# Bias table by matmuls, fewer DMA transposes and another load order in a fused attention and feed-forward kernel

## The chip, the cores and the metric

The kernel runs on one core of a Trainium2 chip. The engines of the core work side by side, each on its own queue of instructions in the order in which the program wrote them: TensorE (PE, matrix products), VectorE (DVE), ScalarE (ACT), GpSimd (POOL) and SyncE (SP). SP and POOL here mostly issue DMAs. The metric is device time in microseconds, the median of several executions.

## The reference

Attention with a relative-position bias, followed by a two-layer network with a squared ReLU. Eight batches, eight heads, 576 positions, head width 64; then 4608 rows of width 512 and a hidden width of 2048.

```python
scores = scale * np.matmul(q, k.transpose(0, 1, 3, 2))        # scale = 1/8
bias = bias_table[bucket]              # bucket depends only on |i - j|; 32 buckets
scores = scores + bias.transpose(2, 0, 1)[None, :, :, :]
scores = scores - np.max(scores, axis=-1, keepdims=True)
attn = np.exp(scores)
attn = attn / (np.sum(attn, axis=-1, keepdims=True) + 1e-09)
attn_out = np.matmul(attn, v)
x = attn_out.transpose(0, 2, 1, 3).reshape(B * S, H * D)
h = np.maximum(x @ w_in, 0.0)
out = h * h @ w_out
```

From a distance of 128 on, all positions fall into the last bucket.

## The kernel before

**Attention, by pairs of heads.** There are 32 pairs, four to a batch (`pair`, L531). Scores are made transposed: keys on the partitions, queries along the row, so that exp(scores) can go into the product with v as the stationary operand. For this q and k must have the head width on the partitions. They are loaded with positions on the partitions (POOL issues these loads, which also convert to 16 bits, by the helper `loader`, L246) and turned in one of two ways. Below batch `DT_QK` = 2 PE turns them with an identity matrix (L559) and ACT or DVE copies the result out of PSUM (L522, L524). From batch 2 on SP issues DMA transposes (L543). Four small copies per pair (L586, on DVE or POOL) put the last 64 queries and keys into block-diagonal tiles `qz` and `kz`. Then PE makes the scores (L604, L628, L653), ACT the exponentials (L615, L638, L663), and PE the product with v (L734, L741); DVE takes the reciprocal of the row sums (L758) and normalises into the tile `x` (L763).

**The bias as a factor.** The bias is not added to the scores. DVE multiplies the exponentials by exp(bias - bias of the last bucket), which is 1 from distance 128 on, so only a band about the diagonal is multiplied (L696). The factors come from two tables with 128 rows, `tb_sb` (384 columns for each head) and `tm_sb` (192 columns for each pair of heads). They are built once at the start: SP loads the bias table, its last row and a one-hot matrix; DVE subtracts (L282), ACT takes the exponential (L285), one matmul makes the 8 x 512 vector of factors by distance (L289), DVE copies it (L296), SP writes it to DRAM and reads it back four times with one element of shift from partition to partition, and DVE copies the reversed rows into the tables (L320, L329).

**From attention to the network.** The network needs x with its 512 features on the partitions, `xt`. With `DT_X` true SP issues two DMA transposes for each pair (L779), three and two blocks of 128 rows. The other way, `x_turn` (L791), stands in the code but isn't used: after all four pairs of a batch, for each of five blocks of rows four PE transposes into one PSUM bank and one copy by ACT or DVE.

**The network, by groups of 512 rows.** Nine groups (`layers`, L830). The first layer is 16 x 4 matmuls of 512 columns (L897), each four followed by a ReLU on ACT (L918) and a square on DVE (L926). The second is 4 x 16 matmuls (L844), with a copy by ACT or DVE (L864, L870) and a store by SP (L878). The second layer of one group is interleaved with the first layer of the next. Both layers, the transposes and the table share three PSUM banks (`g_ps`).

**What sets the order.** The Python program doesn't issue instructions as it meets them. Each step is handed to a planner (`Plan`, L80) with an assumed duration on one or more engines, the steps that it needs, the buffers that it takes from rings, a due time and an earliest time. The planner simulates the engines: at each turn it takes the step that can start first, and by due time among equals; where a step allows two engines, the one that can start it first gets it. The instructions are then issued in the order of the planned starts (L953). So the assumed durations and due times decide which engine gets a copy, and the order of each engine's queue; on the chip the engines follow that order and wait for each other by semaphores. The due times come from `LEAD`, `FAST`, `FASTN` and `PERIOD` (pairs: `nominal`, L506), `AHEAD` (how long before its due time a pair may start) and `G0`, `GP` (groups of the network). DMA transfers are steps on a single planned engine "DMA", and DMA transposes on another, "XB".

**The loads.** POOL issues them in the order in which the program lists them (L481 to L502), as buffers allow: q and k of batch 0 by pairs with v between, the four parts of w_in, batch 1, the four parts of w_out, then batch by batch. q and k have two staging buffers, v has three.

Of the kernel before, what the change touches and what calls it, by code (L numbers as in the profile page):

```python
# [19 lines left out]
NBK = 32  # L20
# [155 lines left out]
def kernel(  # L176
# [17 lines left out]
    oh = np.zeros((NBK, 512), dtype=np.float16)  # L194
    oh[_bucket(np.abs(np.arange(512) - 256)), np.arange(512)] = 1.0
    oh_d = nc.inline_tensor(oh, name="c_oh")
    id_d = nc.inline_tensor(np.eye(128, dtype=np.float16), name="c_id")
    tdram = nc.dram_tensor("t_bias", (H, 512), FP16, kind="Internal")
# [12 lines left out]
    bt_sb = sb("bt_sb", [32, 8], FP32)  # L211
    far_sb = sb("far_sb", [32, 8], FP32)
    eb_sb = sb("eb_sb", [32, 8])
    tv_sb = sb("tv_sb", [H, 512])
    oh_sb = sb("oh_sb", [32, 512])
# [14 lines left out]
    tr_sb = gs[1][:, 0:6, :].rearrange("p a b -> p (a b)").rearrange("p (h w) -> p h w", h=H)  # L230
# [9 lines left out]
    r_set, r_pv, r_g = Ring(2), Ring(1), Ring(3)  # L240
# [5 lines left out]
    def loader(eng_name, eng, out_, in_, packets, deps=(), bufs=(), due=0.0):  # L246

        issue = P.add(
            {eng_name: 800.0 if eng_name == "POOL" else 60.0},
            lambda: io(eng.dma_start(out=out_(), in_=in_())),  # L250
            deps,
            bufs,
            due,
        )
        return P.add({"DMA": packets / 16}, None, [issue], bufs, due), issue
# [8 lines left out]
    nc.scalar.add_instruction(  # L264
        mybir.InstLoadActFuncSet(
            name=nc.get_next_instruction_name(),
            act_func_set_id=tabs.index("natural_log_exp_and_others"),
            ins=[],
            outs=[],
        )  # L270
    )

    l_bt = load("SP", nc.sync, const(bt_sb), const(bias_table), 32 * 27, due=0)
    l_far = load(
        "SP", nc.sync, const(far_sb), const(bias_table[NBK - 1 : NBK, :].to_broadcast([NBK, H])), 32 * 27, due=1
    )
    l_oh = load("SP", nc.sync, const(oh_sb), const(oh_d.ap()), 32 * 60, due=2)
    l_id = load("SP", nc.sync, const(id_sb), const(id_d.ap()), 128 * 27, due=3)

    o = P.add(  # L280
        {"DVE": 150.0},
        lambda: io(nc.vector.tensor_tensor(out=bt_sb, in0=bt_sb, in1=far_sb, op=mybir.AluOpType.subtract)),  # L282
        [l_bt, l_far],
    )
    o_eb = P.add({"ACT": 220.0}, lambda: io(nc.scalar.activation(out=eb_sb, in_=bt_sb, func=EXPF)), [o])  # L285
    bt_b = Buf(r_g)
    o = P.add(
        {"PE": 600.0},
        lambda: io(nc.tensor.matmul(g_ps[bt_b.slot][0:H, :], eb_sb, oh_sb, start=True, stop=True)),  # L289
        [o_eb, l_oh],  # L290
        [bt_b],
        mode="t",
    )
    o = P.add(
        {"DVE": 700.0},
        lambda: io(nc.vector.tensor_copy(out=tv_sb, in_=g_ps[bt_b.slot][0:H, :])),  # L296
        [o],
        [bt_b],
    )
    o = load("SP", nc.sync, lambda: tdram.ap(), const(tv_sb), 16 * 60, [o])  # L300
    l_rev = [
        load(
            "SP",
            nc.sync,
            const(tr_sb[:, 2 * c : 2 * c + 2, :]),
            const(bass.AP(tensor=tdram, offset=2 * c * 512 + 1, ap=[[1, 128], [512, 2], [1, 384]])),
            256 * 50,
            [o],
        )
        for c in range(4)  # L310
    ]
    l_tab = []
    for c in range(4):
        turned = tr_sb[:, 2 * c : 2 * c + 2, ::-1]
        l_tab.append(
            [
                P.add(
                    {"DVE": 900.0},
                    lambda c=c, turned=turned: io(
                        nc.vector.tensor_copy(out=tb_sb[:, 2 * c : 2 * c + 2, :], in_=turned)  # L320
                    ),
                    [l_rev[c]], (), 5000.0 * c,
                )
            ]
            + [
                P.add(
                    {"DVE": 320.0},
                    lambda c=c, e=e, turned=turned: io(
                        nc.vector.tensor_copy(out=tm_sb[ds(64 * e, 64), c, :], in_=turned[0:64, e, 0:192])  # L329
                    ),  # L330
                    [l_rev[c]], (), 5000.0 * c,
                )
                for e in range(2)
            ]
        )
# [57 lines left out]
    def load_six(b, w, h0, nh):  # L393
        src = (q, k)[w]
        l = load(
            "POOL", nc.gpsimd,
            lambda: six(stg[b_stg[b].slot][w])[:, h0 : h0 + nh, :],
            const(src[b, h0 : h0 + nh].rearrange("h (p j) d -> p h (j d)", j=6)),
            96 * nh * 107, (), [b_stg[b]], pdue(),
        )  # L400
        for hp in range(h0 // 2, (h0 + nh) // 2):
            l_qk[b, w, hp] = [l]
# [32 lines left out]
    def load_v_tail(b, hps):  # L435
# [10 lines left out]
    def load_v(b):  # L446
# [9 lines left out]
        load_v_tail(b, range(4))  # L456
# [4 lines left out]
    def load_w_in(u):  # L461
# [5 lines left out]
                512 * 140, (), (), pdue(),  # L467
# [3 lines left out]
    def load_w_out(u):  # L471
# [5 lines left out]
                512 * 140, (), (), pdue(),  # L477
# [10 lines left out]
    for h in range(4, 8):  # L488
        load_v_head(0, h)
    for u in range(4):  # L490
        load_w_in(u)
    for w in range(2):
        load_six(1, w, 0, 4)
    load_v(1)
    for w in range(2):
        load_six(1, w, 4, 4)
    for u in range(4):
        load_w_out(u)
# [13 lines left out]
    def one_of(engs, fn, deps, bufs, due):  # L512
        op = P.add(engs, None, deps, bufs, due)
        op.fn = lambda: fn(op)
        return op

    def copy_to(engs_n, out_f, in_f, deps, bufs, due, fp16=True):


        def emit():  # L520
# [5 lines left out]
        op = P.add(  # L526
            {"DVE": dve(engs_n, 2.0 if fp16 else 1.0, 140.0), "ACT": act(engs_n)}, emit, deps, bufs, due
        )
        return op

    def pair(p):  # L531
# [5 lines left out]
        for w, dst in ((0, qts), (1, kts)):  # L537
            if b >= DT_QK:
# [9 lines left out]
                evac.append(P.add({"XB": 800.0}, None, [o], [qb, b_stg[b]], T - 6000))  # L548
# [29 lines left out]
            evac.append(copy_to(S, straight, turned, [o], [bank, qb], T - 3000, b >= SIX))  # L578
# [116 lines left out]
        def tt(a, t):  # L695
# [6 lines left out]
                [exps[0]] + l_tab[hp], [pb], T,  # L702
# [4 lines left out]
                [exps[1], exps[2]] + l_tab[hp], [pb], T,  # L707
# [4 lines left out]
                [exps[3], exps["q"]] + l_tab[hp], [pb], T,  # L712
# [4 lines left out]
                [exps["k"]] + l_tab[hp], [pb], T,  # L717
# [6 lines left out]
        for part, qt0, nq in ((0, 0, 3), (1, 3, 2)):  # L724
# [49 lines left out]
            if DT_X:  # L774
# [10 lines left out]
                t = x_last[hp, part] = P.add({"XB": 160.0 * nq}, None, [t], [xb], T - 2000)  # L785
# [44 lines left out]
    def layers(g):  # L830
# [76 lines left out]
        for i in range(16):  # L907
            if atoms1:
# [21 lines left out]
                        [r] + ([t for ts_ in l_tab for t in ts_] if g == 1 else []), [rb, gb1], due - 1e5,  # L930
# [55 lines left out]
```

## Time and profile before

| | |
|---|---|
| median of 3 runs | 418.94 us (416.36 to 423.32) |
| the profiled execution, its own time | 420.58 us |
| its span, first to last instruction | 418.6 us |
| PE busy | 378.1 us (90%) |
| ACT / DVE / POOL busy | 263.7 / 197.7 / 152.9 us |
| DMA moved | 42.33 MB, mean 101 GB/s |
| DMA queue of POOL's loads | 102400 packets, 18.36 MB, 58.4% of 16 engines |
| DMA queue of SP | 61360 packets, 23.42 MB, 28.7% of 16 engines |

Times in the profile are microseconds from the start of the span; "mean ns" is nanoseconds. A row of the timeline shows start, duration, engine, line, operation, output and inputs, and in brackets how long the engine had idled before and what it waited for. A row "x21" merges 21 instructions. "SPq" is a DMA instruction in SP's queue. A busy PE isn't a PE at its peak: matmuls overlap, and the array can run at a lower clock. "PEclk" is the clock that the throttle granted; a cold array shows in the spacing of its matmuls.

### The profile page before, as it was taken

Reading aid. Unit: us, or ns where it says so; the run is one execution under the profiler, and the core shown is the slowest. Engines: PE = TensorE matmul, PEld = TensorE weight load, DVE = VectorE, ACT = ScalarE, POOL = GpSimd, SP = SyncE. Lnnn points to the kernel's source line nnn. Section 1 sums busy time; section 2 is a strip of 40 time slices with the busy share of each in tenths; the row PEclk is TensorE's granted clock in tenths of the full one; section 3 lists DMA queues with packets and bytes.
Section 4 is the critical chain, followed back from the end, with each engine's and each line's share of the span. In section 5 each row is a group of like instructions: output and inputs, shape, how many; then the busy total and the mean of one; then the engine's idle time right before and its main releaser. Section 6 shows DMA issues by size and latency. Waiting matters only on the chain.

```text
span 418.6 us, 8453 instructions
## 1 busy us (share of the span) xinstructions
PE 378.1 (90%) x3297; PEld 199.7 (48%) x3297; DVE 197.7 (47%) x540; ACT 263.7 (63%) x374; POOL 152.9 (37%) x242
## 2 busy tenths in 40 slices
PE   4586398687899959999999999999999999999996
PEld 2264144443345435545555587545454545444442
DVE  6475066451364364736563575446543644242200
ACT  4765179651586676866895688578776883564421
POOL 8734469974590148408920494001010000000000
PEclk9998599999899998999999999999999999999999
DMA  9999999999995489939991799442241112100112
GB/s 109 187 200 145 184 131 104 123 119 149 149 100 86 113 110 129 114 70 150 140 131 49 118 136 146 95 100 49 62 117 35 27 33 75 58 0 27 51 52 76
DMA packets 163800, 42.33 MB, mean 101 GB/s; under 512 B 150920, under 2 KB 159152, under 8 KB 163760
## 3 DMA queue, kind: packets, MB, share of 16 engines
q0 software_dynamic: 102400, 18.36, 58.4%
q1 hardware_dynamic: 61360, 23.42, 28.7%
q8 instruction: 26, 0.43, 0.5%
q14 instruction: 14, 0.11, 0.1%
HBM read 37.55 MB, written 9.45 MB: 112 GB/s over the span
## 4 chain that ended last, share of the span: by engine, by line
PE 75%; DMA 13%; POOL 7%; issue 2%; ACT 1%; DVE 1%; SPq 0%; ACTq 0%; POOLq 0%
PE f L844 29%; PE f L897 27%; PE pv L741 8%; PE st L604 6%; DMA va<-in_v_dram 4%; DMA w_out_sb<-in_moe_w_out_dram 4%; POOL va L250 3%; DMA w_in_sb<-in_moe_w_in_dram 3%; DMA xt<-x 3%; PE pv L734 2%; POOL ks L250 2%; PE st L653 1%; PE st L628 1%; POOL qs L250 1%; ACT pt L615 1%
## 5 line engine op out<-in xcount | busy, mean ns | idle before, releaser
L897 PE MATMUL f<-xt,w_in_sb 128*128 128x512 f16 (+1 forms) x640 | 143.4, 367 | 14.3 <-DMA xt<-x 14.1
L615 ACT ACTIVATE pt<-st 128x1024 f16<-128x1024 f32 x128 | 126.0, 1022 | 32.8 <-PE st L604 32.6
L844 PE MATMUL f<-w_out_sb,g 128*128 128x512 f16 x576 | 137.7, 379 | 0.0
L918 ACT ACTIVATE rt<-f 128x512 f16<-128x512 f32 x144 | 85.6, 599 | 61.5 <-PE f L897 59.9
L897 PEld LDWEIGHTS <-w_in_sb 128*128 128x128 f16 x640 | 60.9, 99 | 77.5 <-issue 17.0
L926 DVE TENSOR_TENSOR g<-rt 128x512 f16<-128x512 f16 x144 | 60.2, 421 | 75.8 <-ACT rt L918 74.7
L844 PEld LDWEIGHTS <-g 128*128 128x128 f16 x576 | 53.2, 98 | 64.4 <-issue 8.7
L696 DVE TENSOR_TENSOR pt<-pt,tb_sb 128x512 f16<-128x512 f16 (+2 forms) x96 | 58.4, 621 | 32.8 <-ACT pt L615 31.9
L741 PE MATMUL pv<-va,pt 128*128 128x65 f16 x1280 | 58.2, 197 | 2.8 <-DVE pt L696 2.7
L741 PEld LDWEIGHTS <-pt 128*128 128x128 f16 x1280 | 53.3, 100 | 11.1 <-issue 3.6
L250 POOL DMA_DIRECT2D qs<-in_q_dram x66 | 47.2, 752 | 13.7 <-DMA w_out_sb<-in_moe_w_out_dram 8.2
L250 POOL DMA_DIRECT2D ks<-in_k_dram x66 | 47.5, 793 | 4.4 <-DMA ks<-in_k_dram 3.2
L604 PE MATMUL st<-qt,kt 64*128 64x512 f16 x256 | 42.8, 399 | 5.5 <-ACT pt L615 2.4
L586 POOL COPY qz<-qt 64x64 f16<-64x64 f16 x27 | 7.1, 265 | 99.1 <-DMA qt<-qs 93.4
L734 PE MATMUL pv<-vm,pm 128*128 128x130 f16 x160 | 36.3, 227 | 2.7 <-DVE x L763 2.7
L864 ACT ACTIVATE y<-f 128x512 f32<-128x512 f32 x27 | 16.1, 597 | 34.3 <-PE f L844 33.6
L250 POOL DMA_DIRECT2D va<-in_v_dram x36 | 31.1, 909 | 17.1 <-PE pv L741 14.1
L763 DVE TENSOR_TENSOR x<-pv,r 128x384 f16<-128x384 f32 x64 | 31.3, 489 | 1.8
L758 DVE RECIPROCAL r<-pv 128x6 f32<-128x6 f32 x64 | 12.0, 187 | 42.5 <-PE pv L741 42.1
L663 ACT ACTIVATE pm<-st 128x576 f16<-128x576 f32 x32 | 20.8, 649 | 7.9 <-PE st L653 7.2
L638 ACT ACTIVATE pt<-st 128x512 f16<-128x512 f32 x32 | 19.1, 597 | 5.2 <-PE st L628 4.6
L734 PEld LDWEIGHTS <-pm 128*128 128x128 f16 x160 | 15.9, 99 | 11.4 <-issue 7.1
(42 smaller groups left out, 142.7 us busy)
## 6 DMA issues: line engine op xcount, KB each, us to landing
out_dram<-y SPq DMA_DIRECT2D x36, 256.0 KB, 2.2
va<-in_v_dram POOLq DMA_DIRECT2D x28, 128.0 KB, 5.8
qs<-in_q_dram POOLq DMA_DIRECT2D x48, 64.0 KB, 4.2
ks<-in_k_dram POOLq DMA_DIRECT2D x48, 64.0 KB, 4.0
w_in_sb<-in_moe_w_in_dram POOLq DMA_DIRECT2D x4, 512.0 KB, 11.9
w_out_sb<-in_moe_w_out_dram POOLq DMA_DIRECT2D x4, 512.0 KB, 12.9
xt<-x SPq DMA_TRANSPOSE x64, 3.7
g<-t_bias SPq DMA_DIRECT2D x4, 192.0 KB, 6.9
```

What stands on the lines that cost most here:

```text
L250: lambda: io(eng.dma_start(out=out_(), in_=in_())),
L604: nc.tensor.matmul(sets_ps[st.slot][:, e, :], kt[rw, ts(jt, 128)], qt[rw, 0:512], start=True, stop=True,)
L615: nc.scalar.activation(out=p5(pts[pb.slot])[:, jt, :, 0:512], in_=sets_ps[st.slot], func=EXPF, scale=SCALE)
L663: nc.scalar.activation(out=p4s[pb.slot][:, 0:S].rearrange("p (h s) -> p h s", h=2), in_=sets_ps[st.slot][:, :, 0:HQ], func=EXPF, scale=SCALE,)
L696: io(nc.vector.tensor_tensor(out=a, in0=a, in1=t, op=MULT))
L734: nc.tensor.matmul(ps[:, i, :, :], pm[:, c : c + 128], vm[:, hp, :, 0:65], start=True, stop=False)
L741: nc.tensor.matmul(ps[:, i, e, :], pt[:, (2 * jt + e) * S + c : (2 * jt + e) * S + c + 128], va[:, jt, 2 * hp + e, 0:65], start=False, sto ...
L763: nc.vector.tensor_tensor(out=xs[xb.slot][:, hp, qt0 : qt0 + nq, :].rearrange("p t (e d) -> p t e d", e=2), in0=ps[:, :, :, 0:64], in1=rs[ ...
L844: nc.tensor.matmul(g_ps[bank.slot], gs[gb.slot][:, nt, ts(m, 128)], w_out_sb[:, nt, :], start=(nt == 0), stop=(nt == 15),)
L897: nc.tensor.matmul(g_ps[bank.slot][:, a:z], w_in_sb[:, kk, ts(nt, 128)], xt_sb[:, kk, c : c + z - a], start=(kk == 0), stop=(kk == 3),)
L918: nc.scalar.activation(out=rts[rb.slot], in_=g_ps[bank.slot], func=RELUF)
L926: nc.vector.tensor_tensor(out=gs[gb1.slot][:, nt, :], in0=rts[rb.slot], in1=rts[rb.slot], op=MULT)
```

## The change

Four parts.

1. **Bias table.** The trip through DRAM goes. The bias table is loaded four times, into four groups of 32 partitions, by SP and ACT; the constant becomes four one-hot matrices, shifted by one position each, on 128 partitions. 96 matmuls, each with a 128-column slice of the one-hot rows as the stationary operand and 32 columns moving (4 shifts x 8 heads), make the whole table in six PSUM banks, which ACT or DVE copy to `tb_sb`. Two DVE copies make `tm_sb` from it. The activation table of ACT is now loaded behind ACT's three DMA issues.
2. **DMA transposes later.** q and k are turned by PE up to batch 2 (before: batch 1), x by `x_turn` on PE for batches 0 to 3 (before: never).
3. **Load order.** The eight heads of batch 0's v are spread between its q and k loads; batch 1's v comes behind its q and k.
4. **Planner.** Other constants, other assumed durations for DMA issues and packets; DMA transposes run on the planned "DMA" engine; loads of POOL take one of eight "lanes". The copies of q and k after PE transposes go to DVE alone for pairs 1 to 3.

```diff
-DT_QK = 2
-PERIOD, LEAD, FAST, FASTN = 9800.0, 10600.0, 4700.0, 5
-AHEAD, G0, GP = 12700.0, 38500.0, 37900.0
-DT_X = True
+DT_QK = 3
+PERIOD, LEAD, FAST, FASTN = 9300.0, 7600.0, 4500, 5
+AHEAD, G0, GP = 5600.0, 22900.0, 39300.0
+DT_X = 4
+ORDER = "i0 i1 i2 i3 q0 k0 q1 k1 v o0 o1 o2 o3"
...
-    oh = np.zeros((NBK, 512), dtype=np.float16)
-    oh[_bucket(np.abs(np.arange(512) - 256)), np.arange(512)] = 1.0
+    oh = np.zeros((4, NBK, 512), dtype=np.float16)
+    for i in range(4):
+        oh[i, _bucket(np.abs(252 + i - np.arange(512))), np.arange(512)] = 1.0
...
+        lane = [Buf(r_lane)] if eng_name == "POOL" else []
         issue = P.add(
-            {eng_name: 800.0 if eng_name == "POOL" else 60.0},
+            {eng_name: 720.0 if eng_name == "POOL" else 420.0},
...
+    o_ex = P.add({"ACT": 220.0}, lambda: io(nc.scalar.activation(out=ex_sb, in_=bt_sb, func=EXPF)), [o_bt])
+    o_eb = P.add(
+        {"DVE": 100.0},
+        lambda: io(
+            nc.vector.tensor_tensor(
+                out=eb_sb, in0=sel_sb, in1=ex_sb.rearrange("p (a h) -> p a h", a=1).to_broadcast([128, 4, 8]), op=MULT
+            )
+        ),
+        [o_ex] + z_eb,
...
+    for c in range(6):
+        t_b = Buf(r_g)
+
+        def t_mm(c=c, t_b=t_b):
+            for j in range(16 * c, 16 * c + 16):
+                io(
+                    nc.tensor.matmul(
+                        g_ps[t_b.slot][:, ts(j - 16 * c, 32)], oh_sb[:, 380 - 4 * j : 508 - 4 * j],
+                        eb_sb.rearrange("p i h -> p (i h)"), start=True, stop=True,
+                    )
+                )
+
+        o = P.add({"PE": 16 * 55.0}, t_mm, [o_eb, l_oh], [t_b], LEAD + 500, 0.0, "f")
...
+        tabs_done.append(one_of({"DVE": dve(512), "ACT": act(512)}, t_ev, [o], [t_b], 1.0))
...
-            load_v_tail(0, range(4))
-            for h in range(4):
+            load_v_tail(0)
+        if hp >= 1:
+            for h in range(2 * hp - 2, 2 * hp):
                 load_v_head(0, h)
...
-                evac.append(P.add({"XB": 800.0}, None, [o], [qb, b_stg[b]], T - 6000))
+                evac.append(P.add({"DMA": 1160.0}, None, [o], [qb, b_stg[b]], -1e9))
...
-            evac.append(copy_to(S, straight, turned, [o], [bank, qb], T - 3000, b >= SIX))
+            evac.append(copy_to(S, straight, turned, [o], [bank, qb], T - 3000, b >= SIX, 0 < p < 4))
...
-            if DT_X:
+            if b >= DT_X:
...
-                t = x_last[hp, part] = P.add({"XB": 160.0 * nq}, None, [t], [xb], T - 2000)
+                t = x_last[hp, part] = P.add({"DMA": 232.0 * nq}, None, [t], [xb], -1e9)
...
-        if not DT_X:
+        if b < DT_X:
             x_turn(b, norms)
```

More of the change, by code (lines that the diff above doesn't have):

```diff
@@ L277 @@
[L277 to L308, printed above, removed]
+    l_bt = [
+        load(n, e, const(bt_sb[32 * i : 32 * i + 32, :]), const(bias_table), 32 * 27, due=i)
+        for i, (n, e) in enumerate((("SP", nc.sync), ("SP", nc.sync), ("ACT", nc.scalar), ("ACT", nc.scalar)))
+    ]
@@ L929, in layers @@
                         ),
[L930 removed]
+                        [r], [rb, gb1], due - 1e5,
                     )
```

157 lines of the change are left out of this document (85 added, 72 removed).

## The prediction

> **What bounds the kernel now.** I read the page first: where TensorE (PE) is busy, at what clock, and how full the DMA engines are.
>
> ```profile
> span 418.6 us, 8453 instructions
> ...
> PE   4586398687899959999999999999999999999996
> ...
> PEclk9998599999899998999999999999999999999999
> DMA  9999999999995489939991799442241112100112
> ```
>
> A slice is 10.5 us. From the sixteenth slice on PE shows only nines until the last. Before that it has holes, while the DMA engines are full for twelve slices. So I asked for busy time by stretch:
>
> ```profile
> 0.00:10.00 10.00, 4.75 (x57) 2.58 (x58) 6.11 (x36) 4.75 (x7) 8.84 (x17) 1.00 1.00 108
> 10.00:20.00 10.00, 5.57 (x26) 2.04 (x24) 4.80 (x17) 7.86 (x10) 7.64 (x12) 1.00 1.40 183
> 20.00:30.00 10.00, 9.47 (x146) 7.19 (x147) 7.52 (x27) 5.32 (x7) 4.58 (x6) 1.00 1.24 202
> 30.00:40.00 10.00, 7.10 (x112) 5.09 (x110) 6.30 (x16) 6.66 (x9) 3.20 (x5) 0.92 2.09 150
> 40.00:60.00 20.00, 12.08 (x89) 5.02 (x88) 6.46 (x19) 6.21 (x11) 9.19 (x14) 0.70 1.45 168
> 60.00:80.00 20.00, 15.51 (x188) 8.97 (x187) 12.05 (x29) 16.29 (x25) 19.78 (x31) 1.00 1.65 107
> 80.00:100.00 20.00, 17.94 (x179) 9.82 (x179) 8.45 (x21) 9.67 (x12) 16.10 (x23) 1.00 1.45 121
> 100.00:120.00 20.00, 15.84 (x76) 6.78 (x74) 7.20 (x22) 10.53 (x18) 11.56 (x22) 0.91 1.29 141
> ...
> 140.00:160.00 20.00, 15.23 (x155) 7.90 (x155) 10.54 (x26) 14.13 (x19) 8.55 (x14) 0.95 0.88 113
> 160.00:200.00 40.00, 40.00 (x379) 21.04 (x376) 22.57 (x64) 28.58 (x40) 21.84 (x33) 0.98 1.18 113
> ```
>
> After the stretch, the first columns are its length and the busy time of PE, of its weight loads, DVE, ACT and POOL. The PE idle time in the rows before 160 us adds up: 5.25 + 4.43 + 0.53 + 2.90 + 7.92 + 4.49 + 2.06 + 4.16 + 4.77 = 36.5 us. From 160 us on PE does not wait. So two things count: a hole that closes before 157 us moves the end by its full size, and work added to PE outside the holes costs its full size. The waits of PE name the holes:
>
> ```profile
> PE f L897 <- DMA xt<-x: 14.1, 4, 5.0
> ...
> PE st L653 <- POOL kz L586: 2.9, 1, 2.9
> ...
> PEld L559 <- DMA qs<-in_q_dram: 2.7, 3, 1.4
> ```
>
> The columns are total us, times, longest. The first feed-forward layer (L897) waits for the attention output to be transposed by DMA; loads of q itself are hardly waited for. In order of time, the three hand-overs from attention to that layer, for batches 0, 1 and 2:
>
> ```profile
> 28.73 12.94 SPq L779 DMA_TRANSPOSE xt<-x  x6
> ...
> 39.97 0.43 DVE L763 TENSOR_TENSOR x<-pv,r 128x256 f16<-128x256 f32 x1
> ...
> 48.94 6.20 PE L897 MATMUL f<-xt,w_in_sb 128*128 128x512 f16 x21 [5.00 <-DMA xt<-x]
> ```
>
> ```profile
> 95.53 6.20 PE L844 MATMUL f<-w_out_sb,g 128*128 128x512 f16 x28
> ...
> 95.96 0.42 DVE L763 TENSOR_TENSOR x<-pv,r 128x256 f16<-128x256 f32 x1
> ...
> 97.27 1.29 SPq L542 DMA_TRANSPOSE qt<-qs  x1
> ...
> 99.37 2.11 SPq L779 DMA_TRANSPOSE xt<-x  x1
> ...
> 106.54 3.80 PE L897 MATMUL f<-xt,w_in_sb 128*128 128x512 f16 x9 [4.16 <-DMA xt<-x]
> ...
> 112.80 1.89 PE L897 MATMUL f<-xt,w_in_sb 128*128 128x512 f16 x8
> ```
>
> ```profile
> 152.09 0.42 DVE L763 TENSOR_TENSOR x<-pv,r 128x256 f16<-128x256 f32 x1
> ...
> 156.86 3.08 PE L897 MATMUL f<-xt,w_in_sb 128*128 128x512 f16 x9 [2.18 <-DMA xt<-x]
> ```
>
> Batch 0: the last normalised tile is done at 40.40 us, but SP works through its transposes at 12.94/6 = 2.2 us each, and the matmuls run freely only from 48.94. Batch 1: done at 96.38, the last transpose leaves SP at 99.37 behind another transpose, and lands at 106.5. Batch 2: done at 152.51, first matmul at 156.86. Each time the matmuls after the hole are slow: 9 in 3.80 and 3.08 us, where 8 take 1.89 warm.
>
> **The hand-overs (main gain).** For batches 0 to 3 the change replaces the 32 DMA transposes of x by 80 PE transposes (five groups of four a batch, one PSUM bank and one copy each). The trace has no 128x128 transpose; its nearest rows are the 96x64 ones, cold and warm, and for the copies the evictions of 576 and 512 columns:
>
> ```profile
> 5.04 0.69 PE L559 MATMUL f<-id_sb,qs 96*64 96x96 f16 x12
> ...
> 28.25 0.45 PE L559 MATMUL f<-id_sb,ks 96*64 96x96 f16 x12
> ```
>
> ```profile
> L918 ACT ACTIVATE rt<-f 128x512 f16<-128x512 f32 x144 | 85.6, 599 | 61.5 <-PE f L897 59.9 <-PE st L604 0.8
> ...
> L522 ACT ACTIVATE qt<-f 128x576 f16<-128x576 f16 x5 | 3.3, 651 | 6.5 <-PE f L559 6.4
> ```
>
> A warm twelve takes 0.45 us, 38 ns each; scaled by 128/96 that is 50 ns (cold: 77). A turn of 20 is 1.0 us of PE. Its five copies at 0.60 to 0.65 go over two engines, so three in a row: with the last group's transposes and the hops between engines I take 2.5 us from the last norm to the first matmul. The bounds are 1.5 (only the last copies are left when the norm ends) and 8.1 (each copy queues behind one more job of 1.0 us; priced among the rivals). Then:
>
> - Batch 0: 48.94 - 40.40 = 8.5 us become 2.5, which gives 6.0. The 21 matmuls that took 6.20 us would take 21 x 1.89/8 = 5.0; I count 1.5 with the short runs before it. Together -7.5.
> - Batch 1: the turn, done by 98.9, ends under the 28 matmuls of L844 that run until 101.7. So the hole goes whole, 4.2, and the slow restart with it, 3.80 - 9 x 1.89/8 = 1.7. Together -5.9. Without that cover it would be 2.5 less.
> - Batch 2: 152.51 + 2.5 = 155.0 instead of 156.86, -1.9; the restart costs 3.08 - 2.1 = 1.0 and the cold attention matmuls behind it some 0.7. Together -3.6.
> - Batch 3: no hole before, so none to gain; feed-forward work of earlier groups covers the turn. If that cover is gone, +2.5.
>
> **Batch 2's q and k.** Eight DMA transposes leave SP's queue and 40 PE transposes come, with 8 copies of 0.65 us on ACT or DVE. Nobody waits for these DMAs on PE's list, but POOL's small copies of the transposed tiles sit in the same queue as its load instructions, and one of them held PE for 2.9 us near 77 us. The change makes the planner count at most eight outstanding POOL loads, so its POOL falls behind as the real one does, and I expect it to give this copy to DVE: -2.9, with 0 as the other end, since no line forces it. All PE transposes, 120 x 50 ns, count in full: +6.0 (cold 9.2).
>
> **The bias table.** Removed: one matmul, the trip through DRAM, 12 DVE copies. Added: 96 matmuls with a 128x128 weight load each and 32 columns, six 512-wide evictions, two copies. Where the table was late, and the nearest matmuls:
>
> ```profile
> 4.38 0.58 PE L289 MATMUL f<-oh_sb,eb_sb 32*8 32x512 f16 x1 [4.38 <-DMA oh_sb<-c_oh]
> ...
> 15.20 0.36 DVE L320 COPY tb_sb<-g 128x768 f16<-128x768 f16 x1 [4.04 <-DMA g<-t_bias]
> ...
> 19.06 0.23 PE L741 MATMUL pv<-va,pt 128*128 128x65 f16 x1 [1.49 <-DVE pt L696]
> ...
> 20.40 0.65 PE L741 MATMUL pv<-va,pt 128*128 128x65 f16 x8
> ...
> 29.01 0.40 PE L741 MATMUL pv<-va,pt 128*128 128x65 f16 x8
> ```
>
> By those eights a table matmul costs 81 ns cold or 50 warm: 7.8 or 4.8 us. PE idles 4.43 us between 10 and 20 us and some 0.9 between its first matmul at 4.38 and 10 (5.62 less the 4.75 busy), so 5.3 us hide it and at most 2.5 stick out; against that goes the wait of 1.5 for the table. The six evictions (3.6 us at 0.60) fit into DVE's 5.2 idle us of 10 to 20 us; on ACT, busy 7.86 of 10, they would delay exponentials that PE waits for. The start of the loads stays level:
>
> ```profile
> 0.74 1.28 ACT L264 ACT_TABLE_LOAD   x1 [0.74 <-PEq L970]
> 0.74 0.41 SPq L250 DMA_DIRECT2D bt_sb<-in_bias_table_dram  x1
> ```
>
> Three DMA issues of 0.41 now stand ahead of ACT's table load: 0.74 + 1.2 + 1.28 = 3.2 us, about when the bias arrives. I take 0 for the whole part, ends -2.5 and +3.5. A lower bound below -1.5 is for the clock: PE runs at the cold rate (eights of 0.65) until 28 us, and denser work could warm it earlier.
>
> **Load order and planner constants.** Batch 1's v moves behind its q and k; the same bytes precede batch 2, and PE waited 2.7 us for q in all. Pinning the q and k copies of pairs 1 to 3 to DVE moves at most six 0.65 us jobs off ACT. The due times reorder queues only. 0, ends -4 and +4.
>
> **Sum.** -7.5 - 5.9 - 3.6 - 2.9 + 6.0 + 0 = -13.9 us. The profiled execution took 420.6 us, 2.0 more than its span; 420.6 - 13.9 = 406.7. The median of the runs is 1.6 below the profiled one, so the forecast is **405 us**. The unknown terms (table, order, POOL copy) give this case 397 to 411.
>
> **Rivals.**
> 1. *Loads become the bound.* The DMA row is full to 126 us, so PE, earlier by 8 us after batch 0, could wait for batches 2 and 3 instead. For it: POOL is busy 19.78 of 20 us at 60 to 80 us issuing loads. Against: 40 transposes fewer pass those engines. Then the gains end in new holes and the PE transposes hide in them: about 417 us. Chance 0.15.
> 2. *The transposes keep the array cold.* From 20 to 28 us PE is 95% busy, three bursts of transposes among it, and its eights stay at 0.65 us. If a turn counts as idleness, each restart stays slow (1.5 + 1.7 + 1.7 = 4.9 us not gained) and 120 transposes cost 77 ns, 3.2 more: -5.8, 413 us. Chance 0.12. The Trainium skill speaks for it: "TensorE: Matmul & The Clock Gate", Part 4: PE-mode transpose, says that transposes do not raise the clock and gives some 275 ns for one. By that figure 120 would take 33 us and the whole would come to 432 us as an estimate; the trace's twelve in 0.45 us disagree with the duration, and leave the clock open.
> 3. *The turn is late on its copies (slower).* Engines work in written order. If each of the five copies waits for one exponential (1.0 us) on its engine, a turn takes 5 x 1.6 = 8.1 us with PE waiting in its queue, 5.6 more than counted, four times: +22.4, and the restarts stay cold (+4.9, and 2 for batch 3): 405 + 29 = 434 us. It decides against the change from 3.5 us more per turn. For it: ACT is busy 16.29 of 20 us at 60 to 80. Against: DVE can take copies, and the planner interleaves other matmuls. Chance 0.13.
> 4. *More than counted*: the early clock and the remaining small holes (2.9 at 30 to 40, 2.1 at 80 to 100) close too: under 397. Chance 0.05.
>
> **How the numbers follow.** The forecast's case has 0.55. A measurement of this kernel tells 2% from no change: 410.6 and 427.3 us are the bounds. Faster: nearly all of 0.55, and 0.05 of rival 4, 0.57. Slower: rival 3 and a little of the others' tails, 0.15. Between: 0.28. The range reaches from 395 to 420 and takes in rivals 1 and 2; the forecast's own is 397 to 411.
>
> **What would show it.** In the changed profile L897's waits for transposed x should fall from 14.1 to under 4 us; the first free run of L897 should start by about 43 us and the nines should set in by the twelfth slice. A table matmul's spacing and the x transposes (50 ns) can be read directly. Holes before L897 with a copy as releaser mean rival 3; waits for loaded q, k or v mean rival 1; long cold runs after each turn mean rival 2. The forecast is wrong if PE's idle time before 160 us stays over 28 us, or if PE waits again after it.

## The result, and the profile after

The changed kernel takes 390.6 us (390.4 to 392.2), against 419.1 us for the kernel before: a ratio of 0.935, with a 95% interval of 0.930 to 0.940. The forecast was 405 us, in a range of 395 to 420. The sign was right and the size was not: 28.5 us came off where the sum had 13.9.

The page of the changed kernel (slices are 9.7 us here):

```profile
span 388.6 us, 8835 instructions
...
PE   2877999999999999999999999999999999999995
...
PEclk9999999999999999999999999999999999999999
DMA  7999986979799899799969699999961113001012
```

The nines of PE set in at the fifth slice, not at the sixteenth, and there is no hole behind it. Busy time by stretch, in the columns of the prediction:

```profile
0.00:10.00 10.00, 3.12 (x74) 2.70 (x76) 5.73 (x40) 3.32 (x6) 8.41 (x17) 1.00 0.84 106
10.00:20.00 10.00, 8.45 (x182) 5.80 (x179) 8.49 (x19) 8.51 (x12) 9.71 (x18) 1.00 1.49 151
20.00:30.00 10.00, 7.30 (x119) 4.97 (x116) 7.76 (x19) 9.68 (x13) 6.68 (x12) 1.00 1.22 196
30.00:40.00 10.00, 8.21 (x139) 5.71 (x135) 6.61 (x17) 7.14 (x11) 4.61 (x9) 1.00 1.52 145
40.00:60.00 20.00, 20.00 (x219) 10.74 (x217) 13.66 (x32) 18.03 (x29) 10.94 (x21) 1.00 1.06 129
60.00:80.00 20.00, 20.00 (x207) 11.08 (x203) 11.55 (x31) 12.50 (x16) 11.77 (x17) 1.00 1.10 103
```

PE idles 6.88 + 1.55 + 2.70 + 1.79 = 12.9 us before 40 us, and then not at all up to 360; before it was 36.5 us up to 160. Its busy time fell too, from 378.1 to 371.7 us, although the change adds matmuls. What PE waits for:

```profile
PE f L572 <- DMA id_sb<-c_id: 6.9, 1, 6.9
```

The 14.1 us for x are gone; the longest wait left is the very first, for the identity matrix; every other on the list is at most 1.5 us in all. The hand-over of batch 0, in the timeline:

```profile
35.70 0.42 DVE L776 TENSOR_TENSOR x<-pv,r 128x256 f16<-128x256 f32 x1
...
36.57 0.82 PE L814 MATMUL f<-id_sb,x 128*128 128x128 f16 x8 [0.23 <-ACT qt L534]
...
37.33 0.42 DVE L536 COPY xt<-f 128x512 f16<-128x512 f16 x1
...
37.86 1.90 PE L910 MATMUL f<-xt,w_in_sb 128*128 128x512 f16 x8
```

From the last norm (36.12) to the first matmul of the network it takes 1.7 us, and eight matmuls run in 1.90: warm. The start:

```profile
7.53 0.59 PE L323 MATMUL f<-eb_sb,oh_sb 128*128 128x32 f16 x16
...
8.67 1.03 PE L323 MATMUL f<-eb_sb,oh_sb 128*128 128x32 f16 x32
...
12.80 0.45 PE L572 MATMUL f<-id_sb,qs 96*64 96x96 f16 x12
...
17.20 0.41 PE L754 MATMUL pv<-va,pt 128*128 128x65 f16 x8
```

A table matmul costs 32 ns, and the array is warm from 13 us on (the twelve in 0.45, the eight in 0.41), where it was cold until 28.

### The profile page after: what moved, and what is told of

It reads as the page before. It is cut to its first block, busy times and chain, and to the rows that moved or that the text cites. A ratio compares the mean times of both kernels' runs of the same rounds, so it can differ in the third digit from the quotient of the medians.

```text
span 388.6 us, 8835 instructions
## 1 busy us (share of the span) xinstructions
PE 371.7 (96%) x3512; PEld 202.0 (52%) x3512; DVE 201.1 (52%) x522; ACT 266.4 (69%) x382; POOL 165.6 (43%) x281
## 4 chain that ended last, share of the span: by engine, by line
PE 93%; DVE 2%; ACT 2%; DMA 1%; issue 1%; SPq 0%; ACTq 0%; DVEq 0%
PE f L910 33%; PE f L857 33%; PE pv L754 10%; PE st L617 8%; PE pv L747 3%; PE st L666 2%; PE st L641 2%; DMA id_sb<-c_id 1%; PE f L814 1%; ACT pt L628 1%; PE f L572 1%; PE f L579 1%; DVE pt L709 1%; PE f L323 1%; DVE qt L536 0%
## 5 line engine op out<-in xcount | busy, mean ns | idle before, releaser
L628 ACT ACTIVATE pt<-st 128x1024 f16<-128x1024 f32 x128 | 126.4, 1022 | 38.0 <-PE st L617 37.9
L910 PE MATMUL f<-xt,w_in_sb 128*128 128x512 f16 (+1 forms) x640 | 138.3, 358 | 0.0
L910 PEld LDWEIGHTS <-w_in_sb 128*128 128x128 f16 x640 | 59.2, 98 | 59.1 <-issue 9.3
L754 PE MATMUL pv<-va,pt 128*128 128x65 f16 x1280 | 54.9, 193 | 0.6 <-DVE pt L709 0.6
L754 PEld LDWEIGHTS <-pt 128*128 128x128 f16 x1280 | 50.3, 97 | 5.7 <-DVE pt L709 0.8
L599 POOL COPY qz<-qt 64x64 f16<-64x64 f16 x43 | 12.9, 300 | 80.1 <-DMA qt<-qs 52.9
L617 PE MATMUL st<-qt,kt 64*128 64x512 f16 x256 | 40.1, 385 | 2.8 <-ACT pt L628 1.5
L747 PE MATMUL pv<-vm,pm 128*128 128x130 f16 x160 | 35.4, 221 | 0.3 <-DVE x L776 0.3
L877 ACT ACTIVATE y<-f 128x512 f32<-128x512 f32 x23 | 13.7, 597 | 24.5 <-PE f L857 23.0
L599 POOL COPY kz<-kt 64x64 f16<-64x64 f16 x42 | 13.8, 328 | 38.5 <-DMA kt<-ks 27.5
```

The lines of the kernel that those rows point to most:

```text
L599: io(eng.tensor_copy(out=dst[qb.slot][rw, rw], in_=src[qb.slot][rw, 512:576]))
L617: nc.tensor.matmul(sets_ps[st.slot][:, e, :], kt[rw, ts(jt, 128)], qt[rw, 0:512], start=True, stop=True,)
L628: nc.scalar.activation(out=p5(pts[pb.slot])[:, jt, :, 0:512], in_=sets_ps[st.slot], func=EXPF, scale=SCALE)
L747: nc.tensor.matmul(ps[:, i, :, :], pm[:, c : c + 128], vm[:, hp, :, 0:65], start=True, stop=False)
L754: nc.tensor.matmul(ps[:, i, e, :], pt[:, (2 * jt + e) * S + c : (2 * jt + e) * S + c + 128], va[:, jt, 2 * hp + e, 0:65], start=False, sto ...
L910: nc.tensor.matmul(g_ps[bank.slot][:, a:z], w_in_sb[:, kk, ts(nt, 128)], xt_sb[:, kk, c : c + z - a], start=(kk == 0), stop=(kk == 3),)
```

## The experiments

Each was timed beside the kernel before on the same chip, but not all on one chip: e1 to e4, e5 to e8, e13 to e16, and the others ran on four chips, on which the kernel before took 417.2 to 419.6 us. So a difference of two medians from different groups can be off by some us; where that matters, the text also gives the difference by the ratios. The table gives medians, and ratios to the kernel before with their 95% intervals.

| run | kernel | us | ratio |
|---|---|---|---|
| - | the changed kernel | 390.6 | 0.935 (0.930 to 0.940) |
| e1 | before + turns | 410.2 | 0.976 (0.969 to 0.983) |
| e2 | before + new table | 416.6 | 0.990 (0.981 to 0.998) |
| e3 | before + 96 idle matmuls | 418.3 | 0.994 (0.990 to 0.999) |
| e4 | before + turns + table | 412.3 | 0.980 (0.972 to 0.988) |
| e5 | changed, old due times | 391.7 | 0.940 (0.934 to 0.945) |
| e6 | changed, old load model | 400.2 | 0.959 (0.954 to 0.964) |
| e7 | changed, old table | 396.2 | 0.948 (0.941 to 0.954) |
| e8 | changed, x by DMA | 409.4 | 0.982 (0.976 to 0.989) |
| e9 | e4 + new load model | 393.5 | 0.938 (0.934 to 0.941) |
| e10 | changed, old load order | 391.9 | 0.933 (0.929 to 0.938) |
| e11 | changed, copies not pinned | 394.9 | 0.941 (0.936 to 0.945) |
| e12 | changed, identity loaded first | 395.0 | 0.941 (0.936 to 0.946) |
| e13 | before + new load model | 426.9 | 1.023 (1.015 to 1.031) |
| e14 | e4, small copies on DVE | 404.5 | 0.971 (0.963 to 0.979) |
| e15 | e4 + lanes | 404.5 | 0.970 (0.963 to 0.976) |
| e16 | changed, bias row first | 391.6 | 0.940 (0.934 to 0.945) |
| e17 | e4 + durations | 396.3 | 0.945 (0.940 to 0.950) |
| e18 | changed, q and k of batch 2 by DMA | 396.9 | 0.946 (0.940 to 0.952) |

"Load model" stands for what the change tells the planner of transfers: the eight lanes, the durations of issues and packets, and the DMA transposes as work of the planned DMA engine.

### Parts of the change put into the kernel before

**e1, the turns alone.**

```diff
-DT_QK = 2
+DT_QK = 3
-DT_X = True
+DT_X = 4
-            if DT_X:
+            if b >= DT_X:
-        if not DT_X:
+        if b < DT_X:
```

> The kernel before with part 2 alone: x of batches 0 to 3 and q, k of batch 2 turned by PE; old table, old load order, old planner constants. Theory A (the hand-overs are the gain): 419 less the prediction's terms for hand-overs, plus the transposes, so 401 to 408 us, and L897 waits less than 4 us for x. Theory B (the planner's constants and the load order carry the gain): 414 us or more, new holes in place of the old.

410.2 us, in between. By the ratio this is 10.2 us off (7.2 to 13.2), and L897 waits only 0.4 us, for the copy of `xt`. But there are holes in new places; the stretch of 60 to 80 us in e1:

```profile
60.00:80.00 20.00, 15.96 (x215) 10.47 (x214) 10.95 (x30) 15.08 (x22) 19.96 (x29) 0.83 1.59 102
```

PE idles 4.0 us. POOL has no free moment, but it is on none of PE's waits there: PE waits for ACT's exponentials and DVE's multiplications and norms, inside attention. So the hand-overs are a cause, and something else holds the rest.

**e2, the new table alone** (the table's code as in the change, the planner of before).

> The kernel before with part 1 alone, the table by matmuls; x still turned by DMA. Theory A': the start is a second cause: the table's matmuls warm the array before 15 us instead of 28, attention of batch 0 ends 3 to 7 us earlier, and the whole ends 3 to 7 us earlier, 412 to 416 us. Theory B: the start is covered by the wait for x's transposes, 418 to 420 us.

416.6 us, just above the 412 to 416 of theory A': some 4 us (1 to 8). The array is warm as early as that theory had it (twelve transposes in 0.45 us at 13.7 us), but from 17.1 to 20.4 us it is cold again, and the network still waits 14.7 us for x.

**e3, useless matmuls in place of the table's.**

```diff
+    for c in range(6):
+        w_b = Buf(r_g)
+        def warm(w_b=w_b):
+            for j in range(16):
+                io(nc.tensor.matmul(g_ps[w_b.slot][:, ts(j, 32)], id_sb, id_sb[:, 0:32], start=True, stop=True))
+        P.add({"PE": 16 * 55.0}, warm, [l_id], [w_b], LEAD + 500, 0.0, "f")
```

> The kernel before, with 96 matmuls of 32 columns whose results nobody uses, at the place of the table's matmuls; the table itself still goes through DRAM. If the early clock is what the new table gives, the eights of the attention product fall from 0.65 to 0.40 us before 15 us, and the time is 414 to 417 us. If what counts is that the table is ready earlier, there is no gain: 419 to 422 us.

418.3 us: a gain of 0.6%, about 1% at most, between the two expectations. The timeline of e3:

```profile
12.81 0.42 PE L568 MATMUL f<-id_sb,ks 96*64 96x96 f16 x12
...
15.61 0.61 PE L613 MATMUL st<-qt,kt 64*128 64x512 f16 x4 [2.04 <-ACT kt L531]
17.11 0.61 PE L613 MATMUL st<-qt,kt 64*128 64x512 f16 x2 [0.90 <-ACT pt L624]
...
24.50 0.65 PE L750 MATMUL pv<-va,pt 128*128 128x65 f16 x8
...
26.89 0.40 PE L750 MATMUL pv<-va,pt 128*128 128x65 f16 x8
```

The useless matmuls do warm the array: its twelve transposes run in 0.42 us at 12.8 us, where the kernel before is cold until 28. But then PE waits 2.0 us for a copy of `kt` and 0.9 us for an exponential, and from there it is cold again until 26 us (the two of L613 in 0.61 us, the eights in 0.65). So more matmuls at the start do warm the array, but they don't keep it warm; behind them PE stays thin (4.90 and 5.85 us busy in the first two tens).

**e4, turns and table together.**

> Parts 1 and 2 together on the old planner constants and load order. Theory A with A': the sum of both, 393 to 401 us. Theory B: over 405 us.

412.3 us, over 405 as theory B had it: with both there is no more gain than with the turns alone. Some 22 us (19 by the ratios) are left for the planner, the load order and the pinned copies. In this trace the array is cold until 23 us in spite of the table's matmuls. The trace of e4 shows one hole whole:

```profile
60.08 3.62 POOL L250 DMA_DIRECT2D va<-in_v_dram  x4
63.56 1.40 POOL L250 DMA_DIRECT2D vm<-in_v_dram  x2
64.79 3.70 POOL L250 DMA_DIRECT2D va<-in_v_dram  x4
...
68.29 1.45 POOL L250 DMA_DIRECT2D vm<-in_v_dram  x2
69.78 0.80 POOL L595 COPY qz<-qt 64x64 f16<-64x64 f16 x3
70.52 0.51 POOL L595 COPY kz<-kt 64x64 f16<-64x64 f16 x2
...
71.09 0.66 PE L662 MATMUL st<-qt,kz 128*128 128x288 f16 x2 [5.33 <-POOL kz L595]
71.54 1.91 PE L853 MATMUL f<-w_out_sb,g 128*128 128x512 f16 x4
```

Five copies of 0.25 us stand behind 12 load instructions in POOL's queue; PE waits 5.3 us for them and restarts slowly (4 matmuls in 1.91 us). Before the hole PE had done attention alone, in small steps that wait for ACT.

### Parts taken out of the changed kernel

**e5, the due times of before.**

```diff
-PERIOD, LEAD, FAST, FASTN = 9300.0, 7600.0, 4500, 5
-AHEAD, G0, GP = 5600.0, 22900.0, 39300.0
+PERIOD, LEAD, FAST, FASTN = 9800.0, 10600.0, 4700.0, 5
+AHEAD, G0, GP = 12700.0, 38500.0, 37900.0
```

> The changed kernel with the due times of before (the six planner constants) and all else changed. e4 showed that the table and the turns leave 20 us to be explained by the planner's constants, its model of the loads, the load order and the pinned copies. If the constants carry them (theory P1): 405 to 412 us. If the model of the loads does (theory P2): 391 to 396 us.

391.7 us, as theory P2 had it: in the changed kernel the six constants are worth about 1 us, less than the intervals can tell.

**e6, the load model of before.**

```diff
-        lane = [Buf(r_lane)] if eng_name == "POOL" else []
...
-            {eng_name: 720.0 if eng_name == "POOL" else 420.0},
+            {eng_name: 800.0 if eng_name == "POOL" else 60.0},
...
-                evac.append(P.add({"DMA": 1160.0}, None, [o], [qb, b_stg[b]], -1e9))
+                evac.append(P.add({"XB": 800.0}, None, [o], [qb, b_stg[b]], T - 6000))
```

> The changed kernel with the load model of before: no lanes, the old durations of issues and packets, DMA transposes on their own planned engine. P1: 391 to 396 us. P2: 403 to 412 us, with PE waiting for copies or loads that the plan believed to be there.

400.2 us, 9.6 over the changed kernel and between the two theories. PE's idle time returns at 40 to 100 us (1.4 + 2.5 + 0.4). POOL is at 19.5 of 20 us at 60 to 80 us again, but with loads alone, and it is on none of PE's waits: PE waits for ACT's exponentials and DVE's norms. The comparison with e4 shows more. e6 is e4 with the new due times, load order and pinned copies, and it is 12.1 us faster (8.8 by the ratios). So these are not worth nothing: with the old load model they gain some 9 to 12 us, and with the new one hardly anything (e5, e9).

**e7, the old table in the changed kernel.**

> The changed kernel with the old table through DRAM. If the start counts now that no hand-over hides it: the array stays cold to 20 us or longer and pair 0 waits for the table to 18 us: 396 to 402 us. If the plan absorbs it: 390 to 393 us.

396.2 us: the start is worth 5.6 us here, where it was worth nothing on top of e1. The timeline of e7:

```profile
27.29 0.64 PE L745 MATMUL pv<-va,pt 128*128 128x65 f16 x8
...
33.57 0.64 PE L745 MATMUL pv<-va,pt 128*128 128x65 f16 x8
...
42.71 1.90 PE L901 MATMUL f<-xt,w_in_sb 128*128 128x512 f16 x8
```

The array is cold at 27 us and again at 33, and the network's first free run starts at 42.7 instead of 37.9 us. These 4.9 us reach the end whole: it comes 5.6 us later.

**e8, x by DMA for all batches** (`DT_X = 0` in the changed kernel).

> The changed kernel with x turned by DMA in all batches. If the hand-overs are the largest single part: 401 to 410 us with L897's old waits back. If the new plan hides the DMA turn behind other work of PE: 388 to 394 us, since 80 PE transposes go.

409.4 us: 18.8 us lost. Of PE's waits for x only part returns:

```profile
PE f L910 <- DMA xt<-x: 5.5, 3, 4.2
PE st L617 <- DMA kt<-ks: 3.3, 3, 1.7
```

The rest is spread: PE idles at 40 to 60 us (4.6), and again in small steps as late as 160 to 280 us (2.2 + 1.4 + 2.9). A part is not of the turns: in the profiled execution the array is cold again from 18.5 to 22 us, before any x is turned.

### The planner

**e9, the new load model on e4** (the lines of e6 the other way round, on e4).

> e4 (table and turns on the old planner) with the new load model added: lanes, durations, DMA transposes on the planned DMA engine; constants, load order and copies as before. In e4 PE waits 5.3 us for one POOL copy that stands behind six load instructions. If the model of the loads cures this and its like (theory P2): 392 to 400 us, and the POOL row of 60 to 80 us falls from 19.8 to under 13. If the load order or the pinned copies carry the rest: 404 to 412 us.

393.5 us, as theory P2 had it: 18.8 us (17.8 by the ratios) from a change that adds and removes no step of the computation; it only moves steps within the queues, and some from engine to engine. Its stretch of 60 to 80 us, beneath that of e4:

```profile
60.00:80.00 20.00, 13.11 (x182) 8.05 (x182) 9.50 (x22) 12.35 (x16) 19.82 (x31) 0.83 1.55 99
```

```profile
60.00:80.00 20.00, 20.00 (x192) 10.53 (x189) 11.22 (x28) 11.91 (x16) 9.96 (x16) 1.00 0.91 84
```

POOL falls from 19.8 to 10.0 us, PE rises from 13.1 to 20.0. The timelines of POOL and PE in e9 show how:

```profile
51.60 0.61 POOL L596 COPY kz<-kt 64x64 f16<-64x64 f16 x2 [0.40 <-ACT kt L532]
52.27 0.52 POOL L596 COPY qz<-qt 64x64 f16<-64x64 f16 x2
52.73 0.74 POOL L251 DMA_DIRECT2D qs<-in_q_dram  x1
53.52 0.65 POOL L596 COPY kz<-kt 64x64 f16<-64x64 f16 x2
54.11 3.70 POOL L251 DMA_DIRECT2D qs<-in_q_dram  x5
```

```profile
62.54 0.60 PE L614 MATMUL st<-qt,kt 64*128 64x512 f16 x4
63.08 1.90 PE L854 MATMUL f<-w_out_sb,g 128*128 128x512 f16 x8
64.82 0.41 PE L663 MATMUL st<-qt,kz 128*128 128x288 f16 x2
```

The copies now stand ahead of the loads that follow, and between two steps of attention stand matmuls of the network, which cover ACT's exponentials: PE's list has no wait at all from 45 to 160 us. The same can be counted. Among the kernels with table and turns, the matmuls of the network that PE runs at 60 to 80 us are 12 in e4, 17 in e14, 28 in e15 and in e6, 44 in e17, 56 in e9 and 54 in the changed kernel, and the times fall nearly in that order, from 412.3 to 390.6 us. That is a correlation in one stretch, not a test.

**e13, the new load model alone, on the kernel before.**

> The kernel before with the load model alone: no code of table, turns or order changed. If the model is a gain by itself (a copy held by POOL's loads costs PE 2.9 us in the kernel before): 405 to 414 us. If it only pays once the turns have gone from SP and the DMA engines, because the waits for x's DMA transposes hide it: 417 to 421 us.

426.9 us, slower by 2.3%, outside both expectations. PE's wait for x falls to 2.7 us, but waits for k turned by DMA come in its place, 13.2 us in all. One of them:

```profile
92.77 5.00 SPq L543 DMA_TRANSPOSE kt<-ks  x3
...
96.28 1.03 PE L605 MATMUL st<-qt,kt 64*128 64x512 f16 x4 [7.45 <-DMA kt<-ks]
```

So the model isn't good by itself; without the turns it moves the wait from one set of DMA transposes to the other.

**e14, e4 with the small copies on DVE alone** (`{"DVE": 130.0, "POOL": 300.0}` becomes `{"DVE": 130.0}`).

> e4 (table and turns, old planner) with the small copies of qz and kz on DVE alone, so that none can stand behind loads in POOL's queue; the load model is the old one. If those held copies are what the old model costs: 393 to 400 us. If the model gains by ordering PE or the other queues better: 403 to 411 us (only the 5.3 us wait and its slow restart gone).

404.5 us: 7.8 us less than e4 (3.6 by the ratios), as expected of a gain that isn't the copies alone. PE still idles 4.2 us at 60 to 80 us, now waiting for DVE's norms and ACT's exponentials.

**e15 and e17, the halves of the load model on e4**: the lanes (POOL may have eight loads outstanding in the plan), and the durations with the transposes on the DMA engine.

> e4 with the eight lanes for POOL's loads in the plan, but the old durations and DMA transposes on their own planned engine. If the lanes are what the model gains: 392 to 398 us. If the durations or the transposes on the DMA engine are: 404 to 412 us.

> e4 with the new durations and the DMA transposes on the planned DMA engine, but without the lanes: the other half of the load model. e15 (lanes alone) gave 8 of the 19 us. If the halves add up: 400 to 403 us. If they need each other: 406 to 412 us. If the durations are enough: 393 to 397 us.

404.5 and 396.3 us: 7.8 and 16.0 of the 18.8 us (4.2 and 14.5 of 17.8 by the ratios). So the durations, with the transposes on the DMA engine, carry most of it. Whether the halves overlap or add up can't be told from figures that differ so. With the durations alone, a copy of `qz` is held by POOL's loads once more, for 2.7 us.

### The small parts

**e10, the load order of before.**

```diff
-ORDER = "i0 i1 i2 i3 q0 k0 q1 k1 v o0 o1 o2 o3"
+ORDER = "i0 i1 i2 i3 q0 k0 v q1 k1 o0 o1 o2 o3"
...
-        if hp >= 1:
-            for h in range(2 * hp - 2, 2 * hp):
+            for h in range(4):
```

> The changed kernel with the load order of before (batch 0's v heads in fours, batch 1's v ahead of its second q and k half). If the order is worth nothing, as the prediction took it: 389 to 393 us. If it carries what e5 and e6 leave over: 396 to 402 us.

391.9 us, as the prediction took it: in the changed kernel worth nothing that can be measured.

**e11, the copies of pairs 1 to 3 free to go to ACT** (`0 < p < 4` taken away).

> The changed kernel with the copies of q and k of pairs 1 to 3 free to go to ACT. If the pin is worth nothing: 390 to 392 us. If it keeps ACT free for the exponentials of batch 0: 393 to 396 us, with PE's idle time from 10 to 40 us up from 6.0 us.

394.9 us, 3.0 us more than e10 on the same chip and 4.3 more than the changed kernel. ACT then takes two of the six copies, both of `kt`. No trace shows this kernel at that time, so the reason isn't seen: that the pin keeps ACT free is not shown.

**e12 and e16, other first DMAs on SP**: the identity matrix first (`due=1.7` becomes `due=-1`), and the broadcast row of the bias table first (`due=1.5` becomes `due=-2`).

> The changed kernel with the identity matrix loaded first on SP instead of fourth behind it. PE's first wait in the changed kernel is 6.9 us for that matrix. If the start is on the path: the first transposes start near 5 us and the whole ends 1 to 2 us earlier, 388.5 to 389.5 us. If the bias (its exponential, at 6.65 us) or the loads hold the start: 390 to 391 us.

> The changed kernel with the broadcast of the bias table's last row as SP's first DMA instead of its third. e12 took SP's slots for the identity, pushed this row from 6.45 to 7.02 us and the table with it, and the array was cold again from 18 to 21 us. If the row holds the table: subtraction below 6.2 us, 389 to 390.5 us, or the same as the changed kernel where the identity then comes later. Otherwise 391 to 395 us.

e12: 395.0 us, against both expectations. PE starts at 5.4 us, but the row comes 0.6 us later, and the table with it; then the array, warm at 13 us, is cold again from 18 to 21 us, and the network's first free run starts at 40.3 instead of 37.9 us. Its timeline:

```profile
7.02 0.17 DVE L303 TENSOR_TENSOR bt_sb<-bt_sb,far_sb 128x8 f32<-128x8 f32 x1 [2.12 <-DMA far_sb<-in_bias_table_dram]
...
13.18 0.45 PE L572 MATMUL f<-id_sb,qs 96*64 96x96 f16 x12
...
18.75 0.65 PE L754 MATMUL pv<-va,pt 128*128 128x65 f16 x8
...
22.07 0.41 PE L754 MATMUL pv<-va,pt 128*128 128x65 f16 x8
```

Its four executions go with the clock: 392.6 us at a mean granted clock of 1.000, 395.0 twice at 0.996, and 396.6 at 0.987.

e16: 391.6 us, not to be told from the changed kernel, though PE's first wait falls from 6.9 to 5.7 us and the network's first free run starts at 36.6 instead of 37.9 us. No version ran that beats the change beyond its interval.

**e18, q and k of batch 2 by DMA again** (`DT_QK = 2` in the changed kernel).

> The changed kernel with q and k of batch 2 turned by DMA again, x of batches 0 to 3 still by PE. 40 PE transposes of about 55 ns go, 2.2 us; the prediction took this part as POOL's copy against the transposes, near zero. If the DMA turn is hidden: 388 to 390 us. If PE waits for it: 392 to 396 us, with kt or qt as releaser.

396.9 us, just above the expected 392 to 396, so this part is worth 6.3 us (4.7 by the ratios). PE waits only 0.5 us for `kt`, so the expected releaser isn't it; the idle time is at 80 to 100 us (1.75) and 120 to 140 us (2.1), and the wait for the last norm ahead of `x_turn` rises from 0.7 to 2.0 us. In the profiled execution the array is also cold again from 17 to 21 us.

## Why the prediction was wrong

**What bounds the kernel: right, with one exception.** Holes before 157 us move the end. In e7 4.9 us at the start became 5.6 at the end. But in e16 the network starts 1.3 us earlier, and the span is only 0.5 us shorter.

**The hand-overs: right in kind and in sum.** The terms -7.5, -5.9, -3.6 and +6.0 give -11.0; e1 gives -10.2 (7.2 to 13.2). The single terms were less good: a turn takes 1.7 us, not 2.5; a PE transpose costs 57 ns (9 of them from 34.18 to 34.69 us), not 50. In the full change the same part is worth more: taking out the turn of x costs 18.8 us (e8) and that of q and k 6.3 (e18). That what stands behind a hand-over in the new plan would wait with it is argued, not shown.

**POOL's copy: right that it matters, wrong in the way.** The prediction expected these copies to go to DVE, for -2.9. The groups of before and after:

```profile
L586 POOL COPY qz<-qt 64x64 f16<-64x64 f16 x27 | 7.1, 265 | 99.1 <-DMA qt<-qs 93.4 <-PE st L604 3.3 <-DVE g L926 1.9
L586 POOL COPY kz<-kt 64x64 f16<-64x64 f16 x19 | 5.2, 273 | 17.7 <-DMA kt<-ks 17.0 <-DVE g L926 0.5
```

```profile
L599 POOL COPY qz<-qt 64x64 f16<-64x64 f16 x43 | 12.9, 300 | 80.1 <-DMA qt<-qs 52.9
L599 POOL COPY kz<-kt 64x64 f16<-64x64 f16 x42 | 13.8, 328 | 38.5 <-DMA kt<-ks 27.5
```

POOL makes 85 of them instead of 46. What changed is their place among the loads: PE's list after has no wait for POOL. In e4 one such wait is 5.3 us, and taking all these copies off POOL gave 7.8 us by the medians, 3.6 by the ratios (e14).

**The bias table: taken as 0, ends -2.5 and +3.5.** A table matmul costs 32 ns where the prediction had 50 to 81. Alone it gives about 4 us (e2), on top of the turns nothing (e4), in the full change 5.6 (e7). The lower bound "for the clock" was the right thought and should have had a number: denser work does warm the array, at 13 to 14 us instead of 28 (e2, e3, the changed kernel). What it is worth depends on the plan behind it: in e2 and e3 the array is cold again by 17 us, in e4 it is cold until 23, and with the plan of the change it stays warm.

**Load order and planner constants: here the sum failed.** The prediction wrote "The due times reorder queues only. 0, ends -4 and +4", and it priced the planner's new assumptions on transfers through one copy of POOL alone. These assumptions are the step that failed: put at nothing beyond that copy, they give 18.8 us on top of table and turns (e9), and taking them out of the change costs 9.6 (e6). The two differ because the due times, the load order and the pin do part of the same work: they gain some 9 to 12 us with the old assumptions (e4 against e6) and 1 to 3 with the new ones (e9 against the changed kernel). So the 0 for the due times (e5) and the load order (e10) is shown for the changed kernel only. Planner, order and pin together gain some 19 to 22 us on top of table and turns (e4 against the changed kernel), where the prediction allowed 4 and 2.9 for the copy.

How the assumptions do it is seen in the traces and only in part tested. In the plan of e9, short copies don't stand behind long loads, and the network's matmuls stand between attention's steps. The held copies are not the main thing: e1, e6 and e14 have none on PE's list at 60 to 80 us and still idle there, in waits inside attention. What goes with the time is how many of the network's matmuls stand in that stretch. Whether the new assumptions are nearer to the chip is shown for one only: an issue on SP, planned with 60 and now 420 ns, takes 0.41 us in the trace. The prediction summed the holes that it could name by their releaser and let all others stand; rival 4, that the small ones close too, had the right outcome at a chance of 0.05. The bounds of its own case don't follow from its terms either: the ends that it names for table, order and copy add up to 398.5 and 415.4 us, not to 397 and 411.

**A second reason for the size.** The sum counted idle time and the restarts behind it, and PE's busy time hides more. From before to after the span falls by 30.0 us, of which 23.6 are idle time and 6.4 busy time. e4 and e9 run the same 3512 matmuls, yet PE is busy 381.1 us in e4 and 372.6 in e9: 8.5 of the 18 us of span are not idle time in the profile at all. Part is the slow restarts (in e4, four matmuls in 1.91 us at 71.54, where four take 1.03 at 76.69); that the rest is the spacing of short matmuls that wait for each other is argued, not shown.

**The rivals.** Rival 1 (loads become the bound) did not come: no wait for a load of q, k or v is on PE's list after. Rival 2 (transposes keep the array cold) did not either: eight matmuls of L910 take 1.90 us straight behind a turn. In e1, though, the array is cold in a turn, behind a wait of 0.7 us (eights of 0.65 at 39.9 us). The Trainium skill ("TensorE: Matmul & The Clock Gate", Part 4: PE-mode transpose) gives some 275 ns for one transpose in a kernel. In this trace one takes 219 ns on average (L814), but the next starts after 57 ns, so the prediction's 33 us for 120 counted overlapping times. Rival 3 (late copies) was not seen: ahead of `x_turn` and L910 PE waits under 1 us in all.

**What stays open**: why the pin helps (e11); how much of the load model's gain is PE's order and how much the copies on POOL, beyond the parts that e14, e15 and e17 give; and the clock at the start. That the cold stretch is what e12 loses is likely, since its execution without a lowered clock is its fastest, but no run sets the clock alone.

## What to carry to other kernels

Where a program's order comes from a planner, the numbers that the planner believes are part of the kernel: here 9.6 to 18.8 us came from them with the same steps of computation. Price such an edit by asking which queue holds short work behind long work, and what fills the engine that bounds the kernel while others catch up; and test it together with the code that it was made for, since alone it cost 2.3%. And where several holes have one bound behind them, price "all of them close" as a case of its own: here, once PE had a backlog of the network's matmuls, the small holes went with the large ones.

## What the runs showed of the hardware

- A matmul of 32 columns with 128x128 weights of its own costs 32 ns (32 in 1.03 us), at a time when the twelve transposes beside it still take 0.69 us, the cold rate.
- More matmuls at the start warm the array, and behind a short wait it can be cold again. Without them it is cold until 28 us (the kernel before, e7); with 96 small ones, useful or not, it is warm at 13 to 14 us (e2, e3, the changed kernel), though not in e4. Behind waits of 2.0 and 0.9 us it is cold again in e3. Behind the same wait of 1.09 us for a copy of `kt` it is cold again in e8, e12 and e18, and stays warm in e5, e10, e16 and the changed kernel. The runs don't show why.
- Turning x by DMA makes the changed kernel 18.8 us longer, and PE's list names 5.5 us of it as waits for x and 3.3 as waits for k (e8). So the waits for DMA transposes alone don't give their price.
